# Waiting in the plan for split weights, and stores that follow the planned split, in an adaLN transformer block

## The chip, the cores and the metric

The kernel runs on one core of a Trainium2 chip. The metric is the device time of one execution in microseconds (us), the median of several runs. The engines are TensorE (PE, with its weight loads shown apart as PEld), VectorE (DVE), ScalarE (ACT), GpSimd (POOL) and SyncE (SP). SyncE computes nothing here: it issues all transfers, in order, and stands where a transfer has to wait.

## The reference

One block of a transformer with a conditioning vector c: S = 2048 tokens of D = 576, 32 heads of 18, hidden width 4608, all in float32.

```python
mod = (silu(c) @ w_mod).reshape(1, 6, 1, 576)
sa, ca, ga, sb, cb, gb = mod[:, 0], ..., mod[:, 5]
h = layernorm(x) * (1 + ca) + sa
q, k, v = (h @ wqkv) split into 32 heads of 18
p = softmax(q @ k.T * 18 ** -0.5)
x = x + ga * ((p @ v) @ wo)
h = layernorm(x) * (1 + cb) + sb
x = x + gb * (silu(h @ w1) @ w2)          # w1: 576 x 4608, w2: 4608 x 576
```

## The kernel before

Float32 products are made on PE from two rounded parts, hi and lo, of each operand, in three passes (hi·hi, hi·lo, lo·hi). Weights are split into these parts when they are first loaded.

Attention is done for four blocks b = 0 to 3 of 512 queries, each with 8 groups of 4 heads. One *score step* treats 128 keys (written s in the order below): a product into `psa` (L890) whose row maximum DVE takes (L892), and a product into `psb` (L942) whose exponential ACT takes (L944). The product P·V into `psv` is L979, its result leaves as `ov` and is loaded again as `ou` (L1007). The output projection `psp`, with the low part `tl` made by GpSimd (L1073), the second LayerNorm, the transposes `psT` and the two layers of the MLP are the *filler*: they fill PE between the score steps of the next block. The filler is a list of items, done first in, first out. `hh` and `hl` are the high and low part of the normed, transposed activations (L466 makes `hl`), `g` those after SiLU (L1241). First-layer products are `ps<-hh,w1t` and `ps<-hl,w1t`, second-layer products `ps<-w2t,g`. `gt` and `x` (L1102, L1103) are the result of a second-layer or projection product added to the residual.

The code of the kernel runs a planner, `Plan`, with fixed costs (a score step, a filler item, an operation of DVE, ACT or GpSimd) and a planned time `plan.t`. The string `ORDER` says what PE does next: "s" a score step, "f" the next filler item, a digit n so many key tiles of P·V. An item can have a `need`: a function that gives the planned time from which it can be done, or None; the planner passes to other work until then. The planner does not see the chip; its order is fixed when the kernel is built.

In block 0 the MLP's weights come raw from the input. `load_half` (L746) loads half a tile of 128 rows into one of three `raw` buffers, `split_half` (L771 to L775) lets GpSimd multiply w2's half by the gate gb (L771), cast it to hi (L772; L774 for w1) and subtract to get lo (L775). When both halves are done, the split tile is stored (`store_one`, L782) to scratch memory (`w1s`, `w2s`), from which the later blocks load it (L732). `serve` does at most one of each per planned step: a store when its time has come, a split when the load should have landed (LAND), a load when a buffer is free and the last is some time past (EACH). `split[key]` is GpSimd's planned end of the split of a tile plus 100 ns. `after_pe` ties an instruction to the last PE product before it in the program, so that it does not run ahead of PE.

The second-layer products of the last four tiles of w2 (32 to 35) of a block are held back: `add_mlp2(NFT - CH, left.append)` puts them in the list `left`, and the next block's filler takes them up first, ahead of its projection. For these, `left[0]` has a need of its own, which before is the pair of PSUM banks and the two `g` tiles. The other second-layer items use `weights_need` in block 0.

Of the kernel before, what the change touches and what calls it, by code (L numbers as in the profile page):

```python
# [60 lines left out]
ORDER = (  # L61
    "sssfsssfsssfsss1sss1sss1sss1sss1ss1sssfsssfsssfsss1sss1sss1sssfsssffsss1sss1sss1sss1sss1sss2sss1sssfffsss1sssf"
    "sssfsssfsss1sss1sss1sss1sss1sss2sss1sssfsssffsss1sss1sss1sss1ss1sssfsssfsssfsss1sssfsss2sssffsss1sss1sss1sss1s"
    "ss1sss11sssfsssfsssffsss1sss1sss2sss1sssfsssfsssffsss1sss1sssfsss2sssfffsss1sss1sssfsssfffsss1sss1sss1sss1sss1"
# [3 lines left out]
    "sfsssfsss1sss1sss1sss1sssfss1ss1ss1ss1ss1sssssssssssss1ss1ssss1fss1fss1fss1ssss1sssssssfs1sfs1ss1ssfffsfsfsffs"
    "sffsffsfsffs1sffsfsffffssfffsffffss2sffsfsffsffssffs3sffsfsffssfsffsffsffsffffsfs1sffss1s12sssss1sssss1sss1ssf"
    "fsfsfsfsffssffsfsfsfsffss3sfffssffsffssffsfsfsfsfsf2sfsfsffsfsffssffsfsffssffs21ffffssffsffss1ssffsffssffsfsfs"  # L70
    "1fssfffssffsffss4sfsfsffssffsfsfs11sfsfsfsfsfsffssffsfsfsfsfsfs22sfsffssffsffssffsfsfsffssf2sffffssffsfsf1sfsf"
    "sffssfffssf12fssfffssfffsf1sfsfffssffsfsfs1sfsfsfsfsfsffssffsfsfsfsfsfs22sfsffssffsffssffsfsfsfsfsfs3fsfffssff"
    "sffss1ssffsffssffsffss1sfsfsffssffsfsfs2ssffsffssffsffss21sfsfsfsfsfsffssffsfsfsfffs22fssffsfsfsffssffsfsfsfsf"
    "sfs3fsfffssffsfsfs1ssffsffssffsffss1ssffsffssffsffss2ssffsffssffsfsfs21sfsfsfsfsfsffssffsfsfsfsffs2fffssffffss"
    "ffssffssffsf22sfsfffssffsfsfs1ssffsffssffsfsfs1ssffsffssffsffs2ffffssffsffs1sfsfsffsfffssffsfsfsfsff12fssffsfs"
    "fsffsffsfsfsfsfsf4ffsffssffsffss1ffffssffsffss1ssffsffssffsfsfs2ssffsffssffsfsfs11sfsfsfsfsfsffssffsfsfsfsfsfs"
    "22sfsfsfsfsfsffssffsfsfsfsfsfs31fssfffssffsfsfs1ssffsffssffsfsfs1ssffffssffsfsfs2ssffsffssffsffss12sfsfsfsfsfs"
    "ffssffsfsfsfsffss22sfsffssffsffssffsfsfsfsfsfs21sffffssffsfsfs1ssffsffssffsfsfs1ssffsffssffsfsfs1ssffsffssffff"
    "ss1fffffffssss2ss1ss1fs1sfsfffffsff1sfsfsfsfs1ssffsffssffsfsfs1sfffssffffssfffsfsffsfs2ssffsffssffsfsfs1fsffff"
    "ffssfffsffffss2sfsffsffffssfffffffs1sfffffffssfffsfsfffs1sffffss1ffff11ssss1sss11ssfsffsffsffssffsfsfsfsffss2s"  # L80
    "fsfsffsfsffssffssffsfsffss4ssffsfsfsfsffssffsfsfsfsffss22sffsffssffsfsfs1sffsffssffsfsfs2sffsffssffsfsfs1ssffs"
    "ffssffsfsfs2ssffsfsfsfsffssffsfsfsfsfsf4ssffsfsfsfsffssffsfsfsfsffss22sffsffssffsfsfs1ssffsffssffsfsfs1ssffsff"
    "ssffsfsfs1fssfffssffsffss4ssffsfsfsfsffssffsfsfsfsffss3sfffssffsffssffsfsfsfsffss22fssfffssffffss1sfsfsffssffs"
    "fsfs1sfsfsffssffsfsfs1sfsfsffssffsfsfs2fssffsfsfffssffsffffsf4sfsfsfsfsfsffssffsfsfsfsffss22sffsffssffsfsfs1ss"
    "ffsffssffsfsfs1sfsfsffssffsfsfs3sfsfsffssffsffss2sfsfsfsfsfsffssffsfsfsfsffss1fssffffffssffffffsf4sfsfsffssffs"
    "fsfs2ssffsffssffsfsfs1sfsfsffssffsfsfs1sfsfsffssffsffss4sfsfsfsfsfsffssffsfsfsfsffss22fssfffssfffssffsfsfsfffs"
    "s2sffffssffsff1sfsfsffssffsfsfs2sfsfsffssffsfsfs1sfsfsffssffsfsfs3sfsfsfsfsfsffssffsfsfsfsffss3fssfffsfsffssff"
    "sfsfsfsffs22sfsfffssffffss1fssfffssffsfsfs11ssffsffssffsfsfs1ssffsffssffsfsfs12ssffsfsfsfsffssffsfsfsfsffss2ff"
    "sffsfsffssffsfsfsfsffss3fsfffssffsfsfs1ssffsffssffsfsfs1ssffsffssffffs1ffffssffsffs1fffffffssfss2ss1s1ss1fssff"
    "fffffs1sfsfsffss1ssffsffssffsfsfs1ssfffsffffssfffsfsfffss2ssffsffssffsfsfs1fsfffsfffssfffsffff1fffffffssfffsff"  # L90
    "sffs2sffsfsffffssfffsffffs1ffsffssffs1ff1ssss1ss1s11ssffsfffsffssffsfsfsfsffss21ssfffssffsffssffsfsfsfsffss2sf"
    "fsffssfffssffsfsfsfsffss22fssfffssffsfsfs1ssffsffssffsfsfs1sffsffssffsffss3ssffsffssffsffss2ssffsfsfsfsffssffs"
    "fsfsfsffs2sfsfsffsfsffssffsffssfff3ffffssffff1sffsffssffffs1fsfffssffsffs1ffsffssffsfsfs1sfsffssffsffssfffffss"
    "ffs2fsfffsfsffssffsfsffsff4sfsfsffssffsfsfs1ssffsffssffsfsfs2sfsfsffssffsfsfs1sfsfsffssffsffss4sfsfsfsfsfsffss"
    "ffsfsfsfsffss22fssfffssfffssffsfsffsffs1sffffssffffss1fsfsffssffsfsfs1sfsfsffssffsfsfs4sfsfsffssffsfsfs1sfsfsf"
    "sfsfsffssffsfsffssff4sfsfsfsfsfsffssffsfsfsfsffss3fsfffssffsfsfs1sffsffssffsffss12ssffsffssffsfsfs1sfsfsffssff"
    "sfsfs12sfsfsfsfsfsffssffsfsfsfsffs2fssfffsfsffssffsfsfsfsffss4fssfffssffsfsfs1ssffsffssffsfsfs1sfsfsffssffsfsf"
# [296 lines left out]
def tile_adaln_block(ctx: ExitStack, tc: tile.TileContext, x, wqkv, wo, w1, w2, c, wfirst, wcol, out):  # L394
    nc = tc.nc
# [356 lines left out]
    def split_half():  # L752

        _, ask, h, raw, rel = flight.pop(0)
        key = ask["key"]
# [12 lines left out]
        cs = slice(h * n, h * n + n)
        hi = w[:, 1, cs]
        if gate is not None:  # L770
            after_pe(nc.gpsimd.tensor_tensor(raw, raw, gate[:, cs], op=ALU.mult))  # L771
            nc.gpsimd.tensor_copy(hi, raw)  # L772
        else:
            after_pe(nc.gpsimd.tensor_copy(hi, raw))  # L774
        nc.gpsimd.tensor_tensor(w[:, 0, cs], raw, f(hi), op=ALU.subtract)  # L775
        if h:
            stores.append((plan.t + STORE, w, ask["scr"], ask["key"]))

    def store_one():
# [2 lines left out]
        nc.sync.dma_start(f(scr), f(w))  # L782
# [999 lines left out]
```

## Time and profile before

| | us |
|---|---|
| median of 3 runs | 2374.72 (2371.31 to 2377.79) |
| profiled execution | 2376.84, of which its span 2375.1 |
| PE busy in the span | 2296.8 (97%) |
| DVE, ACT, GpSimd busy | 1767.2, 1476.1, 713.4 |
| granted clock of PE, mean | 0.986 |

The profile names an instruction by line, engine, operation, output and inputs. `idle before` is the time an engine stood before an instruction, and the name behind it the one that released it. SPq stands for SyncE's queue, DMA for a transfer that landed. PEclk is the clock that PE was granted, 1.00 being full. Block 0's MLP runs from about 580 to 1110 us and block 1's begins after it.

### The profile page before, as it was taken

The page shows a single profiled execution, that of the slowest core. Times are in us where ns is not written, and L with a number is a line of the kernel's source. Part 1 is how long each engine was busy: PE and PEld are TensorE (multiplying, and loading weights), DVE is VectorE, ACT ScalarE, POOL GpSimd, SP SyncE. Part 2 cuts the span into 40 slices and gives each one's busy share as a digit, 9 for nine tenths or more (in the row PEclk, how much of TensorE's full clock was granted, in tenths as well). Part 3 has the DMA queues.
Part 4 walks back from the last instruction along what each step waited for, and adds up shares of the span by engine and source line. Part 5 has one row for each costly group of instructions (what it writes and reads, how often), then busy time and mean ns, then how long its engine had stood idle before and what let it go on. Part 6 is the DMA issues. An engine that isn't in the chain of part 4 may idle for free.

```text
span 2375.1 us, 52137 instructions
## 1 busy us (share of the span) xinstructions
PE 2296.8 (97%) x19844; PEld 1580.5 (67%) x19844; DVE 1767.2 (74%) x3089; ACT 1476.1 (62%) x2710; POOL 713.4 (30%) x873
## 2 busy tenths in 40 slices
PE   5999999999899999997999999999999999999999
PEld 4874444444577666774667777776677667778998
DVE  7768889997788887884888888878877888344333
ACT  4237777776577776774577777776766777732121
POOL 5103333314556667664211111112211111110000
PEclk9999999998899999997999999999999999999999
DMA  7455556546466666675545555544654655335653
GB/s 248 160 183 175 176 171 177 172 139 202 160 204 217 213 211 224 208 227 168 190 167 167 192 178 158 189 150 165 224 174 156 196 174 170 131 138 205 219 201 114
DMA packets 201475, 433.02 MB, mean 182 GB/s; under 512 B 31362, under 2 KB 67618, under 8 KB 201226
## 3 DMA queue, kind: packets, MB, share of 16 engines
q1 hardware_dynamic: 201226, 429.68, 54.9%
q8 instruction: 158, 2.59, 0.5%
q14 instruction: 91, 0.75, 0.1%
HBM read 338.54 MB, written 86.33 MB: 179 GB/s over the span
## 4 chain that ended last, share of the span: by engine, by line
PE 87%; DVE 5%; DMA 3%; POOL 2%; ACT 1%; issue 1%; SPq 0%; DVEq 0%; ACTq 0%; POOLq 0%
PE ps L539 26%; PE psv L979 19%; PE psa L890 14%; PE ps L533 10%; PE psb L942 8%; PE psqk L654 4%; DVE mx L892 2%; PE psv L539 2%; PE psp L539 1%; PE psv L1475 1%; PE psqk L539 1%; DMA raw<-in_w 1%; PE psqk L1475 1%; PE psp L533 1%; DMA qt<-qscr 1%
## 5 line engine op out<-in xcount | busy, mean ns | idle before, releaser
L892 DVE TENSOR_REDUCE mx<-psa 128x1 f32<-128x512 f32 x2048 | 1329.8, 684 | 308.5 <-PE psb L942 160.2
L944 ACT ACTIVATE pt<-psb 128x512 f32<-128x512 f32 x2048 | 1149.1, 599 | 501.5 <-PE psb L942 313.9
L942 PE MATMUL psb<-qt,kb 56*128 56x512 f32 x2048 | 750.4, 422 | 3.8 <-ACT pt L944 3.7
L890 PE MATMUL psa<-ka,qt 54*128 54x512 f32 x2016 | 736.8, 419 | 11.6 <-DVE mx L892 9.7
L890 PEld LDWEIGHTS psa<-ka,qt 54*128 54x128 f32 x2016 | 350.3, 187 | 300.0 <-DVE mx L892 172.4
L979 PE MATMUL psv<-pt,vt 128*32 128x512 f32 x4096 | 509.1, 604 | 0.3 <-ACT ov L983 0.3
L539 PE MATMUL ps<-w2t,g 64*128 64x288 f32 x4992 | 419.5, 294 | 20.2 <-POOL w2t L775 12.2
L539 PEld LDWEIGHTS ps<-w2t,g 64*128 64x128 f32 x4992 | 389.0, 186 | 65.0 <-POOL w2t L775 14.8
L942 PEld LDWEIGHTS psb<-qt,kb 56*128 56x128 f32 x2048 | 355.0, 187 | 29.7 <-ACT pt L944 17.6
L539 PE MATMUL ps<-hh,w1t 64*128 64x512 f32 x1944 | 352.9, 395 | 0.0
L1241 POOL TENSOR_TENSOR g<-etmp,g 128x512 fp32r<-128x512 f32 x108 | 138.0, 1297 | 392.6 <-ACT g L1240 366.6
L979 PEld LDWEIGHTS psv<-pt,vt 128*32 128x32 f32 x4096 | 102.7, 109 | 208.2 <-issue 200.9
L539 PEld LDWEIGHTS ps<-hh,w1t 64*128 64x128 f32 x1944 | 194.4, 186 | 48.2 <-issue 5.0
L1103 POOL TENSOR_TENSOR x<-x,gt 128x288 f32<-128x288 f32 x116 | 92.8, 800 | 396.6 <-ACT gt L1102 396.5
L539 PE MATMUL ps<-hl,w1t 64*128 64x512 f32 x864 | 178.5, 392 | 0.0
L1096 DVE TENSOR_TENSOR x<-ps,x 128x288 f32<-128x288 f32 x184 | 83.2, 452 | 109.7 <-PE ps L533 71.5
L533 PE MATMUL ps<-w2t,g 128*128 128x288 f32 x960 | 130.9, 296 | 2.7 <-POOL g L1241 1.4
L533 PEld LDWEIGHTS ps<-w2t,g 128*128 128x128 f32 x960 | 128.6, 188 | 5.5 <-POOL g L1241 1.9
L1237 ACT ACTIVATE eq<-ps 128x512 f32<-128x512 f32 x36 | 21.5, 598 | 146.4 <-PE ps L533 146.4
L533 PE MATMUL ps<-hh,w1t 128*128 128x512 f32 x360 | 106.9, 390 | 0.5 <-DVE hh L468 0.5
L539 PEld LDWEIGHTS ps<-hl,w1t 64*128 64x128 f32 x864 | 89.0, 186 | 16.2
L1238 DVE SCALAR_TENSOR_TENSOR etmp<-etmp 128x512 f32<-128x512 f32 x108 | 77.8, 759 | 13.1 <-ACT etmp L1237 12.3
(150 smaller groups left out, 2134.1 us busy)
## 6 DMA issues: line engine op xcount, KB each, us to landing
w1t<-w1s SPq DMA_DIRECT2D x108, 640.0 KB
w2t<-w2s SPq DMA_DIRECT2D x108, 576.0 KB
kb<-kscr SPq DMA_DIRECT2D x512, 108.0 KB
ka<-kscr SPq DMA_DIRECT2D x504, 108.0 KB
w1s<-w1t SPq DMA_DIRECT2D x36, 640.0 KB
w2s<-w2t SPq DMA_DIRECT2D x36, 576.0 KB
vt<-vscr SPq DMA_DIRECT2D x32, 608.0 KB
qt<-qscr SPq DMA_DIRECT2D x128, 108.0 KB
```

The costliest lines, as they stand in the source:

```text
L533: mm(self.ps[late], lhsT=lhsT, rhs=rhs, start=(i == 0), stop=(i == self.n - 1))
L539: done = mm(self.ps[g], lhsT=lhsT[rows], rhs=rhs[rows], start=(s == 0), stop=(s == self.end))
L654: mm(qk_ps[0], lhsT=w[b][:, kt, :], rhs=(hTl if a else hTh)[:, kt, n * 512:(n + 1) * 512], start=(i == 0), stop=(i == 13))
L890: mm(ps, lhsT=t["q"][64 * j:64 * j + 54, hp, stt * P:(stt + 1) * P], rhs=t["a" if ("a", kc, hp) in t else "b", kc, hp][64 * j:64 * j + 54, ...
L892: return lambda: nc.vector.tensor_reduce(t["mx"][:, 2 * j + hp, stt, kc:kc + 1], ps, axis=AX.X, op=ALU.max)
L942: state["pe"] = mm(ps, lhsT=t["b", kt // 4, hp][64 * e:64 * e + 56, kt % 4 * P:(kt % 4 + 1) * P], rhs=t["q"][64 * e:64 * e + 56, hp, :], s ...
L944: nc.scalar.activation(t["P"][kt, hp][:, e, :], ps, AF.Exp, scale=SCALE)
L979: mm(t["ps"][32 * h:32 * h + 32, :], lhsT=t["v"][:, c0:c0 + 32], rhs=t["P"][kt, h // 2][:, h % 2, :], start=(kt == 0), stop=(kt == NKT - 1 ...
L1096: nc.vector.tensor_add(c["x1"][j][:, hs], ps, c["x1"][j][:, hs])
L1103: nc.gpsimd.tensor_add(c["x1"][j][:, hs], c["x1"][j][:, hs], t)
L1238: nc.vector.scalar_tensor_tensor(t, t, 1.0, u, op0=ALU.add, op1=ALU.mult)
L1241: (nc.vector if last else nc.gpsimd).tensor_tensor(g[:, 1, :], t, f(g[:, 0, :]), op=ALU.subtract)
```

## The change

Three edits. (1) The need of the first held-back product now also asks for the split of the four weight tiles, through `weights_need`. After block 0 this is always satisfied. (2) A store enters the queue with its key; it is issued once the tile's planned split end `split[key]` plus 1500 ns has passed (it was 8000 ns after the split was issued in the plan), and the store is now tied to PE's last product by `after_pe`. (3) The string ORDER is another from position 282 on (205 score steps in).

```diff
-EACH, LAND, STORE = (1500, 2000), 6000, 8000
+EACH, LAND, STORE = (1500, 2000), 6000, 1500
...
         if h:
-            stores.append((plan.t + STORE, w, ask["scr"], ask["key"]))
+            stores.append((key, w, ask["scr"], key))
...
         _, w, scr, _ = stores.pop(0)
-        nc.sync.dma_start(f(scr), f(w))
+        after_pe(nc.sync.dma_start(f(scr), f(w)))
...
-        if stores and stores[0][0] <= plan.t:
+        if stores and split[stores[0][0]] is not None and split[stores[0][0]] + STORE <= plan.t:
             store_one()
...
             add_mlp2(NFT - CH, lambda *a: left.append(a))
-            left[0] = left[0][:3] + (lambda: max(pair_need(), *c["gs"]) if pair_need() is not None and len(c["gs"]) == 2 else None,) + left[0][4:]
+
+            def left_need():
+                return all_ready(pair_need(), *c["gs"], weights_need(*[("w2", NFT - CH + n) for n in range(CH)])) if len(c["gs"]) == 2 else None
+
+            left[0] = left[0][:3] + (left_need,) + left[0][4:]
...
 ORDER = (
     "sssfsssfsssfsss1sss1sss1sss1sss1ss1sssfsssfsssfsss1sss1sss1sssfsssffsss1sss1sss1sss1sss1sss2sss1sssfffsss1sssf"
-    "ss1sss11sssfsssfsssffsss1sss1sss2sss1sssfsssfsssffsss1sss1sssfsss2sssfffsss1sss1sssfsssfffsss1sss1sss1sss1sss1"
+    "ss1sss11sssfsssfsssffsss1sss1sss2sss1sssfsssfsssffsss1sss1sssffffsss1sss1ss1sss1sss1sss1sss1sss1sss1ssfsssfsss"
```

The numbers of instructions on each engine are the same before and after. The P·V products stand in 314 unbroken runs, 311 before.

Where the first held-back product stands on PE (`ps_15542` is its output; an `L979` row with x2 is two P·V products, each `L890`/`L942` pair a score step), before:

```order
L890 MATMUL psa<-ka_80,qt 128x512
L942 MATMUL psb<-qt,kb_89 128x512
L979 MATMUL psv_15447<-pt_2037,vt_2039 32x512 x2
L979 MATMUL psv_15447<-pt_2038,vt_2039 32x512 x2
L890 MATMUL psa<-ka_80,qt 128x512
L942 MATMUL psb<-qt,kb_89 128x512
L890 MATMUL psa<-ka_81,qt 128x512
L942 MATMUL psb<-qt,kb_88 128x512
L539 MATMUL ps_15542<-w2t,g 128x288
L539 MATMUL ps_15543<-w2t,g 128x288
L539 MATMUL ps_15542<-w2t,g 128x288
L539 MATMUL ps_15543<-w2t,g 128x288
```

and after, from five rows further on:

```order
L942 MATMUL psb<-qt,kb_89 128x512
L890 MATMUL psa<-ka_81,qt 128x512
L942 MATMUL psb<-qt,kb_88 128x512
L890 MATMUL psa<-ka_81,qt 128x512
L942 MATMUL psb<-qt,kb_88 128x512
L890 MATMUL psa<-ka_81,qt 128x512
L942 MATMUL psb<-qt,kb_89 128x512
L890 MATMUL psa<-ka_81,qt 128x512
L942 MATMUL psb<-qt,kb_89 128x512
L890 MATMUL psa<-ka_81,qt 128x512
L942 MATMUL psb<-qt,kb_88 128x512
L890 MATMUL psa<-ka_81,qt 128x512
```

Instead of the second-layer products stand further score steps, in all eight in a row. Products `ps<-w2t,g` begin after 18 score steps and 32 P·V products, where it was 9 and 20.

On SyncE, around the loads of the last raw halves (128x288) for that place, before (`vt_2040` is the V tile, `wo` the projection's weights, `w2s<-w2t` the store of a split tile):

```order
L746 DMA raw<-in_w 128x288 x2
L855 DMA ka_82<-kscr 54x512 x2
L746 DMA raw<-in_w 128x288
L782 DMA w2s<-w2t 128x1152
L746 DMA raw<-in_w 128x288 x2
L855 DMA kb_86<-kscr 54x512
L732 DMA wo_15415<-wos 128x1152
L855 DMA kb_86<-kscr 54x512
L862 DMA vt_2040<-vscr 128x1216
L1007 DMA ou<-ov 8x512
L1007 DMA ou<-ov 10x512
L1007 DMA ou<-ov 18x512 x3
```

and after:

```order
L746 DMA raw<-in_w 128x288
L855 DMA ka_82<-kscr 54x512
L782 DMA w1s<-w1t 128x1280
L746 DMA raw<-in_w 128x288
L855 DMA ka_82<-kscr 54x512
L746 DMA raw<-in_w 128x288
L855 DMA kb_86<-kscr 54x512
L746 DMA raw<-in_w 128x288
L855 DMA kb_86<-kscr 54x512
L862 DMA vt_2040<-vscr 128x1216
L732 DMA wo_15415<-wos 128x1152
L1007 DMA ou<-ov 8x512
```

The store that stood between the third and fourth of these raw loads is no longer there; in the new order it comes behind the `ou` loads, after the last row shown. The V tile stands ahead of the projection weights. Another store, of w1, stands between the first raw loads.

On GpSimd, the last splits of w2 and the operations on either side, before:

```order
L1241 TENSOR_TENSOR g<-etmp,g 128x512 x2
L1073 TENSOR_TENSOR tl<-ou,th 128x512
L771 TENSOR_TENSOR raw<-raw,gb 128x288
L772 CAST w2t<-raw 128x288
L771 TENSOR_TENSOR raw<-raw,gb 128x288 x2
L1073 TENSOR_TENSOR tl<-ou,th 128x512
L775 TENSOR_TENSOR w2t<-raw,w2t 128x288
L1073 TENSOR_TENSOR tl<-ou,th 128x512
L772 CAST w2t<-raw 128x288
L1073 TENSOR_TENSOR tl<-ou,th 128x512
L772 CAST w2t<-raw 128x288
L775 TENSOR_TENSOR w2t<-raw,w2t 128x288 x2
```

and after:

```order
L771 TENSOR_TENSOR raw<-raw,gb 128x288
L772 CAST w2t<-raw 128x288
L775 TENSOR_TENSOR w2t<-raw,w2t 128x288
L771 TENSOR_TENSOR raw<-raw,gb 128x288
L772 CAST w2t<-raw 128x288
L775 TENSOR_TENSOR w2t<-raw,w2t 128x288
L771 TENSOR_TENSOR raw<-raw,gb 128x288
L772 CAST w2t<-raw 128x288
L1073 TENSOR_TENSOR tl<-ou,th 128x512
L775 TENSOR_TENSOR w2t<-raw,w2t 128x288
L1073 TENSOR_TENSOR tl<-ou,th 128x512 x3
```

Three of the four L1073 operations moved behind the last subtract L775, and the two L1241 ahead of these splits.

On GpSimd, earlier, at the LayerNorm of block 0's MLP (L441 and L456 belong to the LayerNorm, L466 is hl), before:

```order
L772 CAST w2t<-raw 128x288
L441 TENSOR_TENSOR r_7912<-ve,mhalf 128x1
L775 TENSOR_TENSOR w2t<-raw,w2t 128x288
L456 COPY ob<-ob 128x64
L774 CAST w1t<-raw 128x320
L775 TENSOR_TENSOR w1t<-raw,w1t 128x320
L466 TENSOR_TENSOR hl<-etmp,hh 128x512 x3
L774 CAST w1t<-raw 128x320
L1148 CAST h_8029<-etmp 128x512
L774 CAST w1t<-raw 128x320
```

and after:

```order
L772 CAST w2t<-raw 128x288
L774 CAST w1t<-raw 128x320
L775 TENSOR_TENSOR w2t<-raw,w2t 128x288
L774 CAST w1t<-raw 128x320
L441 TENSOR_TENSOR r_7912<-ve,mhalf 128x1
L775 TENSOR_TENSOR w1t<-raw,w1t 128x320 x2
L774 CAST w1t<-raw 128x320
L456 COPY ob<-ob 128x64
L774 CAST w1t<-raw 128x320
L775 TENSOR_TENSOR w1t<-raw,w1t 128x320
L466 TENSOR_TENSOR hl<-etmp,hh 128x512 x2
L775 TENSOR_TENSOR w1t<-raw,w1t 128x320
```

Casts and subtracts of w1 (128x320) that stood behind the first hl stand ahead of it.

More of the change, by code (lines that the diff above doesn't have):

```diff
@@ L63 @@
     "sssfsssfsss1sss1sss1sss1sss1sss2sss1sssfsssffsss1sss1sss1sss1ss1sssfsssfsssfsss1sssfsss2sssffsss1sss1sss1sss1s"
-    "ss1sss11sssfsssfsssffsss1sss1sss2sss1sssfsssfsssffsss1sss1sssfsss2sssfffsss1sss1sssfsssfffsss1sss1sss1sss1sss1"
-    "sss2sssfsssfsssffsss1sss1sss1sss1sss1ssfsssffsss2sss1sss1sss1sss1sss1fsssfsssfsssffsss1sss1sss1sss2sssfsssfsss"
-    "fsss1sss1sss1fsss1sssfsss2sssffsss1sss1sss1sss1sss1sss1fsssfsssfsssffss1sss1sss2sss1sssfsssfsssfsss1sss1ss1sss"
-    "fsss2sssffsss1sss1sss1sss1sss1sss11sssfsssfsssfsss1sss2sssfsssfsssfsss1sss1sss1sss1sssfsss2sssffsss1sss1sss1ss"
@@ L68 @@
[L68 to L97, printed above, removed]
@@ L98 @@
-    "s1sffsffssfffsf4sfsfsfsfsfsffssffsfsfsfsfsfs2ffsffsfsffssffsfsfsfsff4sfsfsffssffsfsfs1sffffssffffss2sffffssfff"
-    "fss1ffffssffff2fsffffffssfffffsff3fffssffffssffsfffff3ffffssffffs1sffffssffffs12fsfffssffff1sffffssffffs1sffff"
-    "sfffssfffffff4"
+    "ss1sss11sssfsssfsssffsss1sss1sss2sss1sssfsssfsssffsss1sss1sssffffsss1sss1ss1sss1sss1sss1sss1sss1sss1ssfsssfsss"
+    "ffsss1sss1sss2sssfsssfsssfsss1sss1sss1ssffsssfffsss1sss1sss1sss1sss2sss1sssfsssfsssfsss1sss1sss2sss1sss1sss1ss"
+    "s1fsssfsssfsssffsss1sssfsss2sssffsss1sss1sss1sss1sss1sss1fsssfsssfsssffss1sss1sss1sss1sss2sss1sssfsssfsssfsss1"
@@ new lines @@
+    "sssfsss2sssffsss1sss1sss1sss1sss1ssfsssfsss1ssfsss1ss1ss1sssfsss1ss1sssfsssfsss1sss1sss1ssfss1sssffsss1sss1sss"
+    "1sssfsss1ss1sssfsss1sss1sssfss1ss1ss1ss1ss1ssssssssssss1ss1ss1sssf1ss1fss1fss1ssssssss1ss1sfs1sssfs1ssffsffsfs"
+    "ffsfsfsffsfffss1sffsfsffffssfffsffsffs2sffsfsffsffssffsfs21ssfffsfs1sfsffsfsfffffssfffsffsssss1s11fffffss1sss1"
+    "1sssssfffsffssffssffssffsfsffss3ssfffssffsffssffsfsfsfsfsfs12sfsfffssfffssffsfsfsfsffss21fsfffssffsfsfs1ssffsf"
+    "fssffsfsfs1sffsffssffsfsfs3sfsfsffssffsffss3sfsfsfsfsfsffssffsfsfsfsfsfs22sfsffssffsffssffsfsfsfsfsfs12sffffss"
@@ new lines @@
+    "ffsfsfs1sfsfsffssffsfsfs1ssffsffssffsfsfs1sffsffssffsfsfs31sfsfsfsfsfsffssffsfsfsfsfsfs22sfsfsfsfsfsffssffsfsf"
+    "sfsfsfs3fsfffssffffss1sfsfsffssffsfsfs1sfsfsffssffsfsfs3sffsffssffsfsfs2sfsfsfsfsfsffssffsfsfsfsfsfs22sfsfsfsf"
+    "sfsffssffsfsfsfsfsfs3fsfffssffsfsfs1ssffsffssffsffss2ssffsffssffsfsfs1ssffsffssffsffss3sfsfsfsfsfsffssffsfsffs"
+    "ffs22sfsfsfsfsfsffssffsfsfsfsfsfs3sffffssffsfsfs1ssffsffssffsffss2ssffsffssffsfsfs11ssffsffssffsffss2sfsfsfsfs"
+    "fsffssffsfsfsfsffss2fssf21ssffsfsffssffsfsfsfsffss21sffffssffsfsfs1ssffsffssffsfsfs1ssffsffssffsfsfs1sffsffssf"
@@ new lines @@
+    "fsffss21fsfsfsfsfsffssffssffssfffss22sfsffsfsfsffssffffsfsfsfs12fsfffssffsfsfs1sfsfsffssffsffssffsffssffsffss1"
+    "1sffsffssffff1fsffsfsfsffssffffssffsf21fssfffsfffssffsfsfsfsfsf22sfsfffssffsffssffffssffsffssffsffssffffs1fsff"
+    "fssffsfsfs1fffffffssss2ss2ss1ssssssss1fss1fssff1fffffssffffs1sfsfsffssffsfsfs1sffsffsfffssfffsffffss1ssffsffss"
+    "ffsfsfs1fsffffffssfffffff1sffsfffffssfffsffffs1sfffffffssfffsffff1fsfffssffs1ff1ssss1ss1s2ssfffsffssffssffssff"
+    "sfsffss3ssfffssffsffssffsfsfsfsffss2sfsfsffsfffssffsfsffssffs4sfsfsffssffsfsfs1ssffsffssffsfsfs1sffsffssffsfsf"
@@ new lines @@
+    "s13ssffsffssffsfsfs1ssffsfsfsfsffssffsfsffssffs4sfsfsfsfsfsffssffsfsfsfsffss22sffsffssffsfsfs1ssffsffssffsfsfs"
+    "1ssffsffssffsfsfs1sffsffssffsfsfs4ssffsfsfsfsffssffsfsfsfsffss22sfsfsfsfsfsffssffsfsfsfsffss1ffffssffffss2ssff"
+    "sffssffsfsfs1ssffsffssffsfsfs2ssffsffssffsffss2fssffsfsfffssfffssffff4ssffsfsfsfsffssffsfsfsfsffss22sffsffssff"
+    "sfsfs1ssffsffssffsfsfs1ssffsffssffsfsfs2ssffsffssffsffss2ssffsfsffsffssffsffssfffs2fssffffsffssffsfffssff4ssff"
+    "sffssffsffss2ssffsffssffsfsfs1ssffsffssffsfsfs1ssffsffssffsffss4ssffsfsfsfsffssffsfsfsfsffss22sfsfffssfffssffs"
@@ new lines @@
+    "fsfsfsffss21sffffssffsfsfs1ssffsffssffsfsfs1ssffsffssffsfsfs1ssffsffssffsfsfs3ssffsfsffsffssffsfsfsfsffs3sffss"
+    "ffsfsffssffsfsfsfsffs4fssfffssffsfsfs11ssffffssffsfsfs1ssffsffssffsfsfs21ssffsffssffsfsfs1ssffsfsfsfsffssffsfs"
+    "fsfsffs3sfsfsffsfsffssffsfsfsfsffss1ffffssfffsfs2ssffsffssffsffs1sffffssffsffs1fsfffssffffs1ffsfffffsfss2ss1ss"
+    "1ss1ffffs1ffffssffsfsfs1ssffsffssffsffss1ssffsffsfffssfffsfsffsfs2ssffsffssffsfsfs1fsfffsfffssfffsffsff2sfsfff"
+    "fffssfffsffffs1sfffffffssfffsffffs1ffssffsffss1ff1ssss2ss1s1ssffssfffsffssffsfsfsfsffss2sffssffsfffssffsfsfsfs"
@@ new lines @@
+    "ffs3sffssffsfsffssffsfsfsfsffss31ssffffssffsfsfs1ssffsffssffsfsfs1fssfffssffsfsfs22ssffsffssffsfsfs1ssffsfsfsf"
+    "sffssffsfsfsfsff3sffssffsfsffssffsfsffssffs21fsfffssffsfsfs2sfsfsffssffsfsfs1sfsfsffssffsfsfs1sfsfsffssffffs1f"
+    "ffsfsfsffssfffffsff4sfsfsfsfsfsffssffsfsfsfsffss22sfsfffssffsfsfs1ssffsffssffsfsfs1sfsfffssffsfsfs3sfsfsffssff"
+    "sfsfs1sfsfsfsfsfsffssffsfsfsfffs2fssfffsfffssfffffffss1ffffssffffss2ssffsffssffsfsfs1sffsffssfffsf4sffsffssffs"
+    "fsfs1sfffssffsffssffsfsfsfsfsfs3ffsffsfsffssffsfsfsfsffs3fsfffssffsfsfs1sffsffssffsffss2sfsfffssffsfsfs1sfsfsf"
@@ L101 @@
+    "fssffffss3sfsfsfsfsfsffssffsfsfsfsffss3fssffsffsffssffsfsfsfffss3fsfffssffsfsfs1ssffsffssffsfsfs1sfsfsffssffsf"
+    "sfs1ffffssffffs1sfsffffffssffffssfff4sfsfsfsfsfsffssffsfsfsfsffss22sfsfffssffsfsfs1sfsfsffssffsffss2sfsfffssff"
+    "ffss2sffffssffffss12sfsfsfffffssffsffsfff2fsffffffssfffffsff4fsfffssffffss11sffffssffff2fsfffssffffs1ffffssfff"
+    "fs1sfffsffffssfffffff4"
 )
-EACH, LAND, STORE = (1500, 2000), 6000, 8000
+EACH, LAND, STORE = (1500, 2000), 6000, 1500
 QKB = 3
```

## The prediction

> **What bounds the kernel now.** I read the head of the page first, then the waits of TensorE (PE), then the stretch in which the longest of them lie, engine by engine, and at last the clock by stretches.
>
> ```profile
> span 2375.1 us, 52137 instructions
> PE 2296.8 (97%) x19844; PEld 1580.5 (67%) x19844; DVE 1767.2 (74%) x3089; ACT 1476.1 (62%) x2710; POOL 713.4 (30%) x873
> ```
>
> PE is busy for 2296.8 of 2375.1 us. The change alters no product, so PE's work stays; what it can win is the 78.3 us in which PE stands, and the time in which its clock is halved. The waits of PE over the whole run (us in total, times, longest) say who ends that idle time:
>
> ```profile
> PE ps L539 <- POOL w2t L775: 12.2, 3, 9.4
> PE psa L890 <- DVE mx L892: 9.7, 14, 3.3
> PE ps L539 <- POOL w2t L772: 7.6, 4, 5.6
> ```
>
> The first and third row are second-layer products waiting for the GpSimd split of their weights: 19.8 us, of which 15 lie in two single waits. They stand together, at 1091 us, where the products held back from block 0 are done. The groups of that stretch (1090 to 1113 us), and then PE's own timeline:
>
> ```profile
> L539 PE MATMUL ps<-w2t,g 64*128 64x288 f32 x24 | 5.4, 421 | 17.1 <-POOL w2t L775 9.4 <-POOL w2t L772 7.4
> ```
>
> ```profile
> 1081.98 0.40 PE L539 MATMUL ps<-hh,w1t 64*128 64x512 f32 x2
> ...
> 1090.65 0.96 PE L539 MATMUL ps<-w2t,g 64*128 64x288 f32 x12
> ...
> 1097.62 0.61 PE L539 MATMUL ps<-w2t,g 64*128 64x288 f32 x2 [5.64 <-POOL w2t L772]
> ...
> 1110.84 1.35 PE L539 MATMUL ps<-w2t,g 64*128 64x288 f32 x2 [0.98 <-POOL w2t L772]
> ```
>
> PE begins the held-back products at 1090.65 and then stands for 9.4 + 7.4 = 16.8 us, in pieces up to 9.4. The timeline shows no other product in that time. Why GpSimd is late shows on GpSimd (POOL) and on SyncE's queue, which issues the loads:
>
> ```profile
> 1096.29 0.79 POOL L771 TENSOR_TENSOR raw<-raw,gb 128x288 f32<-128x288 f32 x1 [2.90 <-DMA raw<-in_w]
> 1097.14 0.42 POOL L772 CAST w2t<-raw 128x288 fp32r<-128x288 f32 x1
> 1104.11 1.54 POOL L771 TENSOR_TENSOR raw<-raw,gb 128x288 f32<-128x288 f32 x2 [6.54 <-DMA raw<-in_w]
> 1105.60 1.26 POOL L1073 TENSOR_TENSOR tl<-ou,th 128x512 fp32r<-128x512 f32 x1
> ...
> 1110.76 1.54 POOL L775 TENSOR_TENSOR w2t<-raw,w2t 128x288 fp32r<-128x288 f32 x2
> ```
>
> ```profile
> 1074.77 0.36 SPq L746 DMA_DIRECT2D raw<-in_w  x1
> 1081.42 0.35 SPq L782 DMA_DIRECT2D w2s<-w2t  x1
> 1081.88 1.31 SPq L746 DMA_DIRECT2D raw<-in_w  x2
> ...
> 1084.49 0.33 SPq L862 DMA_DIRECT2D vt<-vscr  x1
> ...
> 1093.89 0.37 SPq L746 DMA_DIRECT2D raw<-in_w  x1
> ...
> 1097.59 1.03 SPq L746 DMA_DIRECT2D raw<-in_w  x2
> ```
>
> So GpSimd is late since its raw weights are: the last two halves are issued at 1097.59 and used from 1104.11. SyncE stood from 1074.77 + 0.36 = 1075.13 to 1081.42, 6.3 us, on a store (L782) that waits for a split, and the raw loads and the V tile queue behind it. Then the L1073 operations, 1.26 each, stand between the last casts and subtracts. The clock in the same stretch (PE busy, then PEclk, in two windows):
>
> ```profile
> 1095.00:1107.00 12.00, 0.61 (x2) 0.29 (x2) 0.69 (x1) 1.04 (x2) 4.11 (x6) 0.50 0.67 220
> 1107.00:1118.70 11.70, 9.01 (x43) 5.47 (x45) 1.98 (x3) 1.75 (x3) 5.29 (x7) 0.50 0.25 101
> ```
>
> The clock is half to 1118.7. After the last wait, which ends at 1110.84, that is 7.9 us of work at half speed, and 3.9 us lost. The place costs 16.8 + 3.9 = 20.7 us.
>
> **The change, part by part.**
>
> *Split weights in the plan's condition, and the new order there.* In before 9 score steps and 20 P·V products stand between the end of the first layer (1081.98) and the first held-back product; now 18 and 32. Before, this took 1090.65 - 1082.38 = 8.3 us. The nine more go by the row maximum on VectorE (DVE):
>
> ```profile
> L892 DVE TENSOR_REDUCE mx<-psa 128x1 f32<-128x512 f32 x2048 | 1329.8, 684 | 308.5 <-PE psb L942 160.2
> L979 PEld LDWEIGHTS psv<-pt,vt 128*32 128x32 f32 x4096 | 102.7, 109 | 208.2 <-issue 200.9
> ```
>
> 9 x 0.684 = 6.2 us at least, and nearer 7 with the twelve P·V products between them, so the first held-back product comes at about 1097.6. This is work taken from later, so it costs nothing itself. By my count of the order the fourth tile (35) is first needed some 20 products on: twelve took 0.96 us, so 1.6 us on, at 1099.2.
>
> *Stores after the planned split.* The store now stands behind three more raw loads, the V load and the attention outputs (L1007), and the last half's cast and subtract have one L1073 operation among them instead of three. Two ends bound when the last split is done. Late: the last raw halves come only 6.3 us earlier, at 1104.11 - 6.3 = 1097.8, then two gates (2 x 0.80, half the 1.54 row each), two casts (2 x 0.42), two subtracts (2 x 0.77) and an L1073 (1.26), 5.2 us: 1103.0, a stall of 3.8 us. Early: the ring holds three halves, so the eighth takes the buffer of the fifth, which GpSimd had split before its wait began at 1096.29 - 2.90 = 1093.39; two L1241 operations and an L1073 (1.26 each) stood between, so that buffer was free at about 1089.6. With between 2.4 us (1093.89 to 1096.29) and 6.5 us (1097.59 to 1104.11) to land, and 3.3 us for the half and the L1073, the last split is done between 1095.3 and 1099.4: no stall. I take 1.5 us, since queue and buffers both come free earlier, and keep 0 to 3.8. A store itself hides: SyncE has nothing urgent behind the last one.
>
> So the place falls from 20.7 to 1.5: -19.2 us. No clock loss is counted for a wait that short. The next row shows such a case, at 841 us (the stretch, what ended it, GpSimd just before):
>
> ```profile
> 840.00:842.50 2.50, 0.89 (x9) 0.43 (x5) 0.28 (x1) 0.22 (x1) 2.50 (x4) 1.00 0.20 72
> ```
> ```profile
> PE ps L539 <- POOL w2t L775: 2.4, 1, 2.4
> ```
> ```profile
> 839.85 0.45 POOL L774 CAST w1t<-raw 128x320 fp32r<-128x320 f32 x1 [2.02 <-DMA raw<-in_w]
> ```
>
> A hole of 2.4 us left the clock at 1.00; one of 5.64 us had halved it. The Trainium skill ("TensorE: Matmul & The Clock Gate", Part 1) says that a window of about 3.4 us of idleness halves the clock and about 3.4 us of busy time restores it. Going down agrees with the holes above; coming back does not, as 7.9 us at half speed followed the last wait. By the page the loss here would be 1.7 us and not 3.9, and the forecast 2.2 us higher.
>
> *The same cause elsewhere.* At 841 us a subtract of w2 stood behind a cast of w1 whose raw weights were 2.02 us late. In the new order no w1 split stands between the w2 split and its use at the two tightest places. Ends: 2.4 us won, or as much lost at one of those; I take -1.2.
>
> *P·V.* The runs of P·V go from 311 to 314. A run's start shows as "issue" idle before its weight loads: 200.9 us over 311 runs and their ends is 0.65 a run, 1.9 us for three at most, and PE can hide it all; I take the middle, +0.9.
>
> *Block 0's LayerNorm.* GpSimd had one half split of w1 ahead of the low parts hl; now four. The rows of 592 to 650 us, and the clock there:
>
> ```profile
> L774 POOL CAST w1t<-raw 128x320 fp32r<-128x320 f32 x6 | 2.7, 451 | 7.3 <-PE psb L942 4.5 <-PE psa L890 2.8
> L775 POOL TENSOR_TENSOR w1t<-raw,w1t 128x320 fp32r<-128x320 f32 x5 | 4.2, 866 | 0.2
> ```
> ```profile
> 633.00:647.00 14.00, 13.79 (x52) 5.41 (x54) 10.54 (x18) 6.64 (x12) 7.60 (x11) 0.53 0.41 135
> ```
>
> Three more halves are 3 x (0.45 + 0.87) = 4.0 us ahead of hl at most. Against it, fewer score steps stand between the transposes and the first layer (10 for 14), 4 x 0.68 = 2.7 us, and the half clock (0.53 over 14 us) may shift. Ends -4 and +4; I take 0. The projections of Q and K (312 to 540 us) are also in another order; PE is full there, and I put 0, with 3 us either way.
>
> Sum against the profiled execution (2376.84; 1.74 outside its span, 2.1 above the runs' median of 2374.72): 2376.84 - 19.2 - 1.2 + 0.9 = 2357.3. Forecast 2357. From the median it would be 2355.
>
> **The rivals.**
>
> *The loads stay half late.* For it: the V load and others still share SyncE's queue with the raw loads, and the last landing took 6.5 us. Against it: the store that held all of them for 6.3 us stands behind them now. A stall of about 6 instead of 1.5 us, with half the clock loss (2): 2364. If the raws land no earlier than 1104.11, the split ends at 1104.1 + 5.2 = 1109.3, the stall is 10.1, and the clock loss stays: 2376.84 - 6.7 - 0.3 = 2370, too little to tell from no change. That is also the case in which the plan's condition does not do what it says, since it goes by planned, not by real ends.
>
> *A new hole at block 0's LayerNorm.* 4.0 us of splits ahead of hl, and a second stretch like that of 633 to 647, 14 x (1 - 0.53) = 6.6 us: 2357 + 10.6 = 2368.
>
> *More is won.* The same half-clock stretch does not come in the new order: 2357 - 6.6 = 2350. For it: PE had hardly a gap there (13.79 of 14 us busy), so the clock is lost to something the order may move. Against it: nothing in the new order there is plainly lighter.
>
> *Slower: stores stand too close behind GpSimd.* SyncE's waits for stores, over the run:
>
> ```profile
> SPq L782 <- POOL w2t L775: 49.0, 22, 7.5
> SPq L782 <- POOL w1t L775: 14.1, 10, 3.4
> ```
>
> A store used to go out 8 us of the plan after its split was issued; now 1.5 us after its planned end. Where GpSimd runs behind the plan, SyncE waits for longer, and raw loads behind it turn late, as at 1075. Each hole so made costs about 12.2 / 3 = 4.1 us and 3.9 us of clock. From four such holes on, 32 us, the gain of 19.5 turns into a loss beyond what can be told: 2357 + 32 = 2389. Against it: 72 stores had only 32 waits, 2 us each in the mean (63.1 us in all).
>
> **How the numbers follow.** About 0.3%, 7 us, is what a measurement of this kernel can tell from no change. Forecast (2351 to 2363): 0.53. More won (2350): 0.10. Half late (2364): 0.15. Fully late (2370): 0.08. New hole (2368): 0.08, half of it beyond 0.3%. Slower: 0.06. Faster is 0.53 + 0.10 + 0.15 + 0.04 = 0.82, same 0.12, slower 0.06. The range runs from 2347 (the gains of 841 and of LayerNorm in full, no stall: 2357 - 1.5 - 1.2 - 4, and the 3 us of Q and K) to 2370, leaving out the slower case and the tails.
>
> **What would show it.** In the new profile the waits of PE for w2t should fall from 19.8 to under 6 us, with no single one over 4, and the granted clock be 1.00 at about 1100 us. SyncE's V load should go out at about 1075 to 1078 and the last raw halves before 1093. Waits of SyncE for stores should not exceed 63 us by much. The forecast is wrong if a wait of over 5 us stands at the held-back products, if psT or the first layer of block 0 waits over 4 us near 630 us, or if the half-clock stretches grow in number.

## The result, and the profile after

| | before | after |
|---|---|---|
| median, us | 2373.98 (4 runs, 2371.31 to 2377.79) | 2353.98 (4 runs, 2352.55 to 2355.56) |
| profiled span, us | 2375.1 | 2353.8 |
| granted clock, mean | 0.986 | 0.990 |

The ratio of the times is 0.9915, with a 95% interval of 0.9898 to 0.9932: 20 us less (16 to 24), where 2357 and a gain of 19.5 had been forecast. The waits of PE over the whole run, after; the rows for w2t that were 12.2 and 7.6 us:

```profile
PE psT L1142 <- DVE ob L455: 5.0, 2, 3.9
...
PE ps L539 <- POOL w2t L775: 1.6, 1, 1.6
...
PE ps L539 <- POOL w2t L772: 0.8, 1, 0.8
```

Both w2t waits that are left lie at 1050 us, none at the held-back products. New is 3.9 us of a transpose (psT) waiting for the LayerNorm. PE's timeline at the held-back products, after:

```profile
1078.96 0.43 PE L539 MATMUL ps<-hh,w1t 64*128 64x512 f32 x2
...
1097.87 1.86 PE L539 MATMUL ps<-w2t,g 64*128 64x288 f32 x24
...
1100.03 1.75 PE L539 MATMUL ps<-w2t,g 64*128 64x288 f32 x24
```

These 48 run without a wait, and PE waits for w2t at none of the held-back products behind them. SyncE and GpSimd there:

```profile
1073.79 0.32 SPq L862 DMA_DIRECT2D vt<-vscr  x1
...
1081.32 0.35 SPq L782 DMA_DIRECT2D w2s<-w2t  x1
...
1085.28 0.55 SPq L746 DMA_DIRECT2D raw<-in_w  x1
1085.92 0.70 SPq L782 DMA_DIRECT2D w2s<-w2t  x1
1086.71 0.83 SPq L746 DMA_DIRECT2D raw<-in_w  x1
```

```profile
1093.06 0.80 POOL L771 TENSOR_TENSOR raw<-raw,gb 128x288 f32<-128x288 f32 x1 [4.17 <-PE psv L979]
...
1097.68 0.80 POOL L775 TENSOR_TENSOR w2t<-raw,w2t 128x288 fp32r<-128x288 f32 x1
1098.44 4.23 POOL L1073 TENSOR_TENSOR tl<-ou,th 128x512 fp32r<-128x512 f32 x3
```

The last raw half goes out at 1086.71, not behind 1097.59. GpSimd stands for 4.17 us ahead of the next gate, by this trace for PE, to whose place in the program the split is tied. In a second trace of the same kernel (e10 below) the landing of the load released the same instruction:

```profile
1089.51 0.80 POOL L771 TENSOR_TENSOR raw<-raw,gb 128x288 f32<-128x288 f32 x1 [3.49 <-DMA raw<-in_w]
```

Counted from the end of the first layer this is 14.0 us, for 13.7 in the kernel after: load and PE come at nearly the same time here, and the load still bears on the end of the splits. The last split ends at 1098.48, just behind PE's arrival, and three of the L1073 operations stand behind it.

To see where the 21.3 us of the two spans come from, I counted PE's products in both traces and took the times at which the same number of them, of the same kinds to within two products, had begun:

| products begun | place | before | after | difference |
|---|---|---|---|---|
| 2085 | order still the same | 312.4 | 314.3 | +1.9 |
| 3684 | Q and K done | 573.6 | 577.3 | +3.8 |
| 4660 | behind the LayerNorm of block 0 | 701.1 | 699.5 | -1.6 |
| 8376 | last first-layer products of block 0 | 1082.0 | 1079.0 | -3.0 |
| 9120 | some 60 us behind the held-back products | 1181.3 | 1159.1 | -22.3 |
| 18176 | order the same again | 2093.8 | 2073.0 | -20.9 |
| 19839 | end | 2370.1 | 2349.3 | -20.9 |

Between 8376 and 9120 lie 19.3 of the 21 us. PE's idle time falls there by 17.4 us (19.9 to 2.5), its busy time by 1.8 (79.4 to 77.6). The 1.9 us up to 312 us are chance, since PE's order is the same there; the other kernels' traces, with the same order up to there, stand between -3.7 and +1.8 us against before at that point.

### The profile page after: what moved, and what is told of

Its sections match the earlier page's. It is cut to its first block, busy times and chain, and to the rows that moved or that the text cites. A ratio compares the mean times of both kernels' runs of the same rounds, so it can differ in the third digit from the quotient of the medians.

```text
span 2353.8 us, 52121 instructions
## 1 busy us (share of the span) xinstructions
PE 2293.4 (97%) x19844; PEld 1580.8 (67%) x19844; DVE 1768.1 (75%) x3089; ACT 1473.9 (63%) x2710; POOL 712.2 (30%) x873
## 4 chain that ended last, share of the span: by engine, by line
PE 86%; DVE 6%; DMA 3%; ACT 2%; issue 1%; POOL 1%; SPq 0%; DVEq 0%; ACTq 0%; POOLq 0%
PE ps L539 26%; PE psv L979 18%; PE psa L890 14%; PE ps L533 10%; PE psb L942 8%; PE psqk L654 3%; DVE mx L892 2%; PE psv L539 2%; DMA qt<-qscr 1%; PE psp L539 1%; PE psv L1479 1%; DMA raw<-in_w 1%; PE psqk L539 1%; PE psqk L1479 1%; PE psp L533 1%
## 5 line engine op out<-in xcount | busy, mean ns | idle before, releaser
L942 PE MATMUL psb<-qt,kb 56*128 56x512 f32 x2048 | 744.9, 421 | 3.5 <-ACT pt L944 3.5
L890 PE MATMUL psa<-ka,qt 54*128 54x512 f32 x2016 | 734.4, 418 | 11.9 <-DVE mx L892 9.3
L890 PEld LDWEIGHTS psa<-ka,qt 54*128 54x128 f32 x2016 | 348.6, 186 | 306.3 <-DVE mx L892 170.1
L979 PE MATMUL psv<-pt,vt 128*32 128x512 f32 x4096 | 510.1, 604 | 0.3 <-ACT ov L983 0.3
L539 PE MATMUL ps<-w2t,g 64*128 64x288 f32 x4992 | 412.5, 293 | 3.0 <-POOL w2t L775 1.6
L942 PEld LDWEIGHTS psb<-qt,kb 56*128 56x128 f32 x2048 | 352.2, 186 | 26.4 <-ACT pt L944 15.7
L1241 POOL TENSOR_TENSOR g<-etmp,g 128x512 fp32r<-128x512 f32 x108 | 137.4, 1292 | 386.6 <-ACT g L1240 349.4
L979 PEld LDWEIGHTS psv<-pt,vt 128*32 128x32 f32 x4096 | 102.3, 109 | 210.6 <-issue 202.5
```

What stands on the lines that cost most here:

```text
L539: done = mm(self.ps[g], lhsT=lhsT[rows], rhs=rhs[rows], start=(s == 0), stop=(s == self.end))
L890: mm(ps, lhsT=t["q"][64 * j:64 * j + 54, hp, stt * P:(stt + 1) * P], rhs=t["a" if ("a", kc, hp) in t else "b", kc, hp][64 * j:64 * j + 54, ...
L942: state["pe"] = mm(ps, lhsT=t["b", kt // 4, hp][64 * e:64 * e + 56, kt % 4 * P:(kt % 4 + 1) * P], rhs=t["q"][64 * e:64 * e + 56, hp, :], s ...
L979: mm(t["ps"][32 * h:32 * h + 32, :], lhsT=t["v"][:, c0:c0 + 32], rhs=t["P"][kt, h // 2][:, h % 2, :], start=(kt == 0), stop=(kt == NKT - 1 ...
L1241: (nc.vector if last else nc.gpsimd).tensor_tensor(g[:, 1, :], t, f(g[:, 0, :]), op=ALU.subtract)
```

## Experiments

The theories: *order* (the new place of the products, splits and loads wins the time), *queue* (it is the store that no longer heads SyncE's queue), and the waiting of the plan by itself. All kernels are told by what they change in the kernel after or before; each ratio is against the kernel before on the same chip (medians 2373.28 to 2375.53).

**The waiting.** With the old need for `left[0]` in the kernel after, the program that is built is the same, instruction for instruction: as the order is written out, and it stands late enough, the condition never holds anything up. So it needs no run there. In the old order it moves some issues on SyncE and GpSimd. e6 is the kernel before with this alone:

```diff
-left[0] = left[0][:3] + (lambda: max(pair_need(), *c["gs"]) ..., ) + left[0][4:]
+left[0] = left[0][:3] + (left_need,) + left[0][4:]
```

> The kernel before with the plan's waiting for the split weights alone (old order, old stores). The order of PE is written out, so waiting moves only what SyncE and GpSimd do around it. All theories that put the gain into order or stores: 2371 to 2376 us, no change. Theory 'the plan's waiting itself starts the loads in time': a stall of less than 8 us, 2362 to 2368 us.

2374.09 us, ratio 0.9996 (0.9983 to 1.0009). No change, with 16.7 us of waits at the place in its trace. The waiting wins nothing in itself; it can only have steered the search for the order.

**The stores.** e1 has the new store rule in the kernel before, e2 the old store rule in the kernel after:

```diff
# e1, to the kernel before
-EACH, LAND, STORE = (1500, 2000), 6000, 8000
+EACH, LAND, STORE = (1500, 2000), 6000, 1500      # with its three lines in split_half, store_one, serve
# e2, to the kernel after
-EACH, LAND, STORE = (1500, 2000), 6000, 1500
+EACH, LAND, STORE = (1500, 2000), 6000, 8000      # with the three old lines
```

> The kernel before with the new store rule alone (old order, no waiting for the split weights). Theory 'queue' (the gain at the held-back products comes from the store leaving the head of SyncE's queue): the raw halves go out earlier, about half of the 16.8 us stall goes, 2364 to 2366 us. Theory 'order' (the gain comes from the work that now stands ahead of the held-back products and of the last splits): the store still stands ahead of the V load and waits for its split, GpSimd's last splits still stand between the L1073 operations, the stall stays over 13 us and the time at 2371 to 2375 us.

> The kernel after with the store rule of before (new order, waiting for split weights). Theory 'order': no wait of over 3 us at the held-back products, 2352 to 2357 us. Theory 'queue': the stall of 10 us or more is back, 2365 to 2372 us.

e1: 2366.72 us, ratio 0.9968 (0.9952 to 0.9984). e2: 2351.51 us, ratio 0.9899 (0.9882 to 0.9917). In the old order the stores alone won 8 us, as *queue* had it, but not where it had it: the place still lost 13.9 us. Part of the rest was won ahead of the place. From product 4660 to 8376 (701 to 1082 us) the two traces with old order and old stores (before, e6) took 380.8 and 384.6 us, the four with old order and new stores (e1, e3, e8, e9) 377.3 to 378.2. In the new order the stores win nothing: there it was 377.6 us in both traces with the old stores (e2, e11) and 379.0 to 381.9 in the five with the new ones. e10 and e11 put the two store rules side by side in the new order:

> The kernel after once more, beside e11 on the same chip: 2352 to 2356 us.

> The kernel after with the old store rule, beside e10. If the new store rule is worth something in the new order: slower than e10 by 2 us or more. If not: within 2 us of it, or faster.

e10: 2352.56 (2351.77 to 2357.71); e11: 2349.61 (2349.21 to 2357.03). Not slower, so the new store rule is not what the gain rests on.

Why the stores alone help so little shows on e1's engines (PE, then GpSimd):

```profile
1084.58 0.96 PE L539 MATMUL ps<-w2t,g 64*128 64x288 f32 x12
...
1098.31 0.85 PE L539 MATMUL ps<-w2t,g 64*128 64x288 f32 x3 [9.74 <-POOL w2t L775]
```

```profile
1095.50 0.79 POOL L771 TENSOR_TENSOR raw<-raw,gb 128x288 f32<-128x288 f32 x1 [1.30 <-DMA raw<-in_w]
1096.24 1.26 POOL L1073 TENSOR_TENSOR tl<-ou,th 128x512 fp32r<-128x512 f32 x1
...
1098.21 1.27 POOL L1073 TENSOR_TENSOR tl<-ou,th 128x512 fp32r<-128x512 f32 x1
...
1099.81 1.26 POOL L1073 TENSOR_TENSOR tl<-ou,th 128x512 fp32r<-128x512 f32 x1
...
1101.40 1.54 POOL L775 TENSOR_TENSOR w2t<-raw,w2t 128x288 fp32r<-128x288 f32 x2
```

The last raw half lands for 1095.50, and then three L1073 operations stand between the last casts and subtracts. e9 takes just these from GpSimd in e1:

```diff
-eng = nc.vector if last and kt % 2 == 0 or b and kt == 4 else nc.gpsimd
+eng = nc.vector if last and kt % 2 == 0 or b and kt == 4 or b == 1 and kt < 4 else nc.gpsimd
```

> The kernel of e1 (new stores, old order), with the four low parts of block 1 (L1073) on VectorE instead of GpSimd. In e1 the last raw weights go out at 1087.7 and the last split still ends at 1102.9, with three L1073 operations of 1.26 us between the last casts and subtracts. If GpSimd's queue sets the end of the splits by then: it ends 3.8 us earlier, the stall falls from 13.9 to about 10 us, 2361 to 2364 us. If the landing of the loads sets it: no change, 2366 to 2368 us.

2362.68 us, ratio 0.9949 (0.9929 to 0.9968). Counted from the end of the first layer the last split ends 3.2 us earlier than in e1 (24.1 for 27.3) and the stall is 11.4 instead of 13.9 us. The intervals of the two ratios overlap (e1's ends at 0.9952), so it is the traces that show this: GpSimd's queue is part of the cause, and by then a small one.

**Which part of the order.** e3 is the old order up to two score steps ahead of the end of block 0's first layer and the new one from there; e4 the reverse; e8 the new order only over 59 score steps from that point, with the held-back products in them, and the old one before and after. The other edits are in.

> Old order up to the last first-layer product of block 0 (two score steps ahead of it), new order from there; both other edits in. Theory 'order': the 19.3 us of the held-back products are won, those of the LayerNorm (about 4 us net) are not: 2355 to 2360 us. Theory 'queue', in which the loads far ahead of the place matter: less, 2362 to 2368 us.

> The counterpart: new order up to that point, old order behind it; both other edits in. The V load and the first raw halves stand ahead of the waiting store here, as in the kernel after. Theory 'queue': the held-back products wait 3 us at most, about 2356 us. Theory 'order': PE arrives nine score steps earlier and the L1073 operations stand between the last splits again, a stall of 8 to 15 us and half the clock: 2366 to 2372 us.

> Old order up to the held-back products, new order over them alone (39 to 60 score steps), old order after; both other edits in. Theory 'order', with the place as the only one that matters: 19 us from there and 5 to 7 us from the new stores in the first part, none lost later: 2348 to 2353 us. If the first part's 5 to 7 us was chance, or the new order's LayerNorm is worth 4 us: 2355 to 2358 us.

e3: 2358.06, ratio 0.9929 (0.9910 to 0.9948). e4: 2365.71, ratio 0.9961 (0.9949 to 0.9973). e8: 2354.86, ratio 0.9919 (0.9902 to 0.9936). New order over one place of some 60 us gives about the total of the whole new order, though not by the place alone: between products 8376 and 9120 e8 takes 84.6 us, where before took 99.4 and after 80.1, and the rest of its gain lies ahead of the place, where its order is the old one. e4 has the V load and the first raw halves ahead of the store, as after, and waits 12.8 us all the same:

```profile
1088.87 0.96 PE L539 MATMUL ps<-w2t,g 64*128 64x288 f32 x12
...
1100.02 0.61 PE L539 MATMUL ps<-w2t,g 64*128 64x288 f32 x2 [9.82 <-POOL w2t L772]
1103.11 0.85 PE L539 MATMUL ps<-w2t,g 64*128 64x288 f32 x4 [2.48 <-POOL w2t L775]
```

**Distance or readiness.** e5 is the kernel after with the first 24 held-back products put ahead of twelve of the score steps:

```diff
# cut out of one line of ORDER
-ssss2ss2ss1ssssssss1fss1fssff1fffffssffffs1
+ssss2ss2ss1fffffffffssssssss1ss1ss1ssffffs1
```

> The kernel after, but its first four items (24 products) of the held-back products stand ahead of twelve score steps and twelve P·V products that stood before them; PE gets there about 9 us earlier, at 1088 to 1089 us. Theory 'distance' (PE must come late enough for the last splits; the loads are early now but not that early): the last split ends at 1095 to 1097, a wait of 4 to 6 us plus 2 to 4 us of clock, 2359 to 2363 us. Theory 'readiness' (with loads and splits early and the L1073 operations behind them, the extra steps are not needed): a wait of 2 us at most, 2352 to 2356 us.

2375.18 us, ratio 0.9996 (0.9985 to 1.0008): the whole gain is gone, more than either theory said. PE there, then GpSimd:

```profile
1079.49 1.19 PE L539 MATMUL ps<-w2t,g 64*128 64x288 f32 x13
1090.17 0.61 PE L539 MATMUL ps<-w2t,g 64*128 64x288 f32 x2 [9.49 <-POOL w2t L772]
1096.54 2.35 PE L539 MATMUL ps<-w2t,g 64*128 64x288 f32 x9 [5.76 <-POOL w2t L775]
```

```profile
1090.08 1.26 POOL L1073 TENSOR_TENSOR tl<-ou,th 128x512 fp32r<-128x512 f32 x1
...
1091.67 2.48 POOL L1073 TENSOR_TENSOR tl<-ou,th 128x512 fp32r<-128x512 f32 x2
...
1094.48 1.26 POOL L1073 TENSOR_TENSOR tl<-ou,th 128x512 fp32r<-128x512 f32 x1
1095.70 2.29 POOL L775 TENSOR_TENSOR w2t<-raw,w2t 128x288 fp32r<-128x288 f32 x3
```

The edit moved more than products: on GpSimd all four L1073 operations (5.0 us) now stand ahead of the last subtracts, where the kernel after has one. So the case that *readiness* asked for, splits early and L1073 behind them, was not run, and e5 undoes two things at once. The last split is done 6.0 us later than in the kernel after (25.1 for 19.1); without that the wait of 15.3 us would have been about 9, by an estimate from these two numbers.

All kernels in one table, in us from the end of block 0's first layer (from their timelines of PE, SyncE and GpSimd):

| | last raw half issued | last split done | PE at first held-back product | wait |
|---|---|---|---|---|
| before | 16.2 | 29.9 | 8.3 | 16.8 |
| e6 (waiting) | 16.2 | 30.4 | 8.9 | 16.7 |
| e1 (stores) | 12.4 | 27.3 | 8.9 | 13.9 |
| e9 (e1, L1073 on VectorE) | 13.3 | 24.1 | 8.8 | 11.4 |
| e4 (order until there) | 18.2 | 24.5 | 8.3 | 12.8 |
| e5 (products earlier) | 8.9 | 25.1 | 6.6 | 15.3 |
| e3 (order from there) | 12.2 | 22.5 | 18.7 | 1.9 |
| e8 (order there alone) | 12.5 | 22.5 | 19.0 | 1.6 |
| e2 (old stores) | 7.7 | 19.6 | 15.6 | 2.0 |
| e11 (old stores again) | 8.3 | 19.2 | 16.9 | 0.6 |
| e7 (new order until later) | 8.7 | 19.2 | 17.0 | 0.6 |
| after | 8.1 | 19.1 | 18.5 | 0 |
| e10 (after again) | 8.9 | 19.8 | 18.2 | 0 |

The wait is the time from PE's arrival (third column) to the last split (second), less some 2 to 5 us of products that need only the earlier tiles. No kernel has the splits done before 19 us; every kernel in which PE comes at 6 to 9 us waits 11 us or more, and every one at 15 or later 2 us at most.

An earlier split and a later arrival count alike. e9 and e8 have the last split done at nearly the same time (24.1 and 22.5), PE comes 10.2 us later in e8, and the wait is 9.8 us shorter. before and e9 have PE at nearly the same time (8.3 and 8.8), the split is done 5.8 us earlier in e9, and the wait is 5.4 us shorter. From before to after the split is done 10.8 us earlier and PE comes 10.2 us later. Against a wait of 16.8 us either alone would have left 6 to 7 us, by an estimate from these numbers; no run has splits at 19 us with PE at 8, or splits at 30 us with PE at 18.

**A splice that lost.** e7 follows the new order for 1436 score steps, to about 1470 us, and the old one from there.

> The kernel after up to block 2 (score step 1436 of the order), the old order behind it. In the traces the kernels with the new order lose 1.5 to 2.8 us between about 1400 us and the end of block 2 against the old one. If that loss belongs to the order: 2351 to 2353 us. If it is chance: 2354 us.

2381.55 us, ratio 1.0021 (1.0008 to 1.0034), which neither case had foreseen. PE's waits between 1470 and 1620 us, where it loses 28 us against the kernel after:

```profile
PE ps L539 <- DVE x L1096: 9.6, 10, 1.1
PE ps L539 <- ACT etmp L1230: 3.9, 4, 1.2
```

The products of both layers wait for VectorE and ScalarE to empty the banks. A likely reason, which no run shows, is that the shares of score steps and products between the banks' turns no longer fit behind the seam. Half of the 28 us are such waits; what the rest is stays open. The new order itself does lose there, which was the question of this run: between products 9120 and 18176 the six traces with the new order (after, e2, e3, e5, e10, e11) took 913.8 to 913.9 us, the six with the old one (before, e1, e4, e6, e8, e9) 912.3 to 912.5, so it costs 1.4 us.

## Why the prediction was right, point by point

- *Held-back products, -19.2 us.* Measured -19.3 (products 8376 to 9120), and that this is so close is luck, for two parts were off and cancel. PE's idle time fell by 17.4 us, where 15.3 had been forecast (16.8 to 1.5), mostly since the wait was put at 1.5 us and is 0. Its busy time fell by 1.8 us, where 3.9 of lost clock had been forecast to go: no clock loss was counted for the longer stretch of score steps, which had one. PE comes at 18.5 us behind the first layer's end, where 15.2 had been forecast, and the rows of the clock say why:

```profile
1085.00:1090.00 5.00, 4.74 (x24) 2.12 (x23) 4.39 (x8) 3.99 (x8) 3.75 (x5) 0.98 0.93 250
1090.00:1095.00 5.00, 5.00 (x23) 1.51 (x23) 3.01 (x5) 3.11 (x7) 1.79 (x3) 0.50 0.93 361
1095.00:1100.00 5.00, 5.00 (x48) 2.71 (x42) 1.86 (x4) 3.01 (x6) 4.94 (x7) 0.84 0.53 207
```

  In e2, whose clock stayed at 1.00 there, PE comes at 15.6 us and waits 2.0 us, close to the 15.2 and 1.5 of the forecast.
- *The cause of the earlier splits.* Here the prediction named the wrong edit. It put the earlier loads down to the stores that follow the planned split; e2 has the old rule and its last raw half at 7.7 us, as early as in the kernel after (8.1). So the order alone moves them that far; the stores alone move them from 16.2 to 12.4 us (e1). The sum was not touched, since the times were read from the order as built.
- *The hole at 841 us, -1.2.* It is gone, and 2.4 us (0.8 and 1.6) came instead at 1050 us: 0.
- *P·V, +0.9.* Not to be told apart; the order behind product 9120 costs 1.4 us in all.
- *Block 0's LayerNorm, 0 (from -4 to 4).* Measured -5.4 (products 3684 to 4660), beyond that end, and both of its mechanisms came. The hole of the rival is there: LayerNorm's L441 stands behind a cast of w1 whose raw weights are late (GpSimd, VectorE):

```profile
625.49 0.45 POOL L774 CAST w1t<-raw 128x320 fp32r<-128x320 f32 x1 [1.57 <-DMA raw<-in_w]
625.90 0.55 POOL L441 TENSOR_TENSOR r<-ve,mhalf 128x1 f32<-128x1 f32 x1
```

```profile
626.49 0.81 DVE L447 TENSOR_TENSOR t<-r 128x1 f32<-128x1 f32 x1 [2.81 <-POOL r L441]
```

  It makes the wait of 3.9 us at psT, just short of the 4 us that were to be a sign against the forecast. Against it the half clock of 634 to 642 us did not come, though two shorter stretches did, at 629 and 643 us:

```profile
634.00:642.00 8.00, 6.25 (x38) 1.92 (x30) 8.00 (x14) 5.07 (x9) 7.85 (x8) 1.00 0.19 57
```

  Over the same products the seven traces with the new order there (after, e2, e4, e5, e7, e10, e11) took 117.8 to 123.8 us, in the mean 121.6, and the six with the old one 123.2 to 127.6, in the mean 125.4. So some 4 us belong to the order, and what one trace shows is largely chance.
- *Q and K, 0 (3 either way).* 1.9 us in these two traces, by the table above, and not by chance: the same seven traces took 262.8 to 264.5 us from product 2085 to 3684, the six with the old order 260.5 to 262.4.
- *The slower rival.* SyncE's waits for stores did not grow: the rows of 2 us or more sum to 42.7 us after and to 71.0 before, and most of the 42.7 are for PE, to which a store is now tied:

```profile
SPq L782 <- PE psb L942: 20.4, 16, 3.5
SPq L782 <- PE psa L890: 9.0, 12, 1.5
SPq L782 <- POOL w2t L775: 5.2, 2, 3.8
```

- *The small terms together, -0.3.* The table gives -1.6 outside the place: +3.8 up to the end of Q and K, -5.4 at the LayerNorm, -1.4 from there to the place, +1.4 behind it. That they nearly cancel is luck too.
- *The signs.* The V load went out at 1073.79 (1075 to 1078 had been given), the last raw half ahead of 1093, and the w2t waits fell to 2.4 us (under 6). Two signs came out otherwise. The clock at about 1100 us, which was to be 1.00, was 0.84 from 1095 to 1100 us and 1.00 from 1100 to 1105. And the stretches at half clock did grow in number, from 8 to 11 by the clock records of the two traces, though their sum fell from 68 to 48 us.
